# Second products of weight pairs run once for two token tiles, in products of 512 columns

## The chip, the cores and the metric

The program runs on one core of one Trainium2 chip. The core has five engines that run side by side and wait for each other through semaphores: TensorE (PE in the profile, its weight loads PEld), VectorE (DVE), ScalarE (ACT), GpSimd (POOL) and SyncE (SP), which issues the DMAs. The metric is the device time of one execution in microseconds (us); less is better.

## The reference

```python
# attention in chunks of 32 with 16 keys to the left, 8 to the right and 8 memory keys -> x [1536, 512]
# first layer: 4 experts, d = 512, f = 1024
p = domain_probs / (domain_probs.sum(-1, keepdims=True) + 1e-09)
for e in range(4):
    h = np.maximum(x @ w1[e], 0.0)
    out += p[:, e:e + 1] * (h @ w2[e])
# second layer: d = 512, f = 2048
h = x @ w_in
g = np.maximum(h, 0.0) + alpha * np.minimum(h, 0.0)
return (g @ w_out)
```

Everything is float32.

## The kernel before

The kernel keeps activations transposed: rows are features, columns are tokens. The 1536 tokens are two halves, a = 0 and a = 1, of 768 columns each (`NCOL`). A *token tile* is 384 columns of both halves, so there are two tiles, that with `c0 = 0` and that with `c0 = 384`. The hidden features come in 24 groups of 256, called p below: p = 0 to 15 are the experts of the first layer, four groups each, p = 16 to 23 are the second layer. Attention (12 units) runs ahead of and between the first tiles.

For each p and tile there are two products.

- The **first product** (`gemm1`) is a matrix product by seven block products (a scheme of the Strassen kind): groups of six matmuls into the PSUM banks a, b, d, a, c, d, c, 42 matmuls of 384 columns. Float32 is split in a high and a low part, and three matmuls (high by high, high by low, low by high) make one product. VectorE combines the banks between groups: `u`, `t`, `b`, `d`, `c` in the rows. The second c group adds into bank c, which VectorE must have read before (row `b<-c,t`).
- Then comes the nonlinearity (`gelu`), once for each of four blocks of the hidden features (i = 0, 1 by half a = 0, 1; block 2i+a), in the order 0, 3, 1, 2. It ends in an ACT cast that makes the high half of `gg` and a POOL subtraction that makes its low half (`gg<-g,gg`). In the second layer two ACT operations stand ahead of VectorE's.
- The **second product** (`gemm2`) multiplies the four blocks by the second weights: for each of four output blocks o and each half a, two features halves i by three matmuls, into one bank `y`; 48 matmuls of 384 columns. VectorE adds each bank to the accumulator `acc` (row `acc<-y,acc`).

Four groups around the change of layer (p = 14 to 17) go through `gemm2_two`, which already runs two p after two first products. The order of the program is the list `order`: (1, k) is the first product of tile k of the list `tiles`, (2, k) its second. For the other groups the list puts a first product ahead of the second product of the tile before it, as (1, k), (2, k-1).

Everything else is placed by hand into this order: a planner keeps a time `now`, which each matmul moves on, and generators (streams) emit a step when `now` reaches its due time. The streams are the preparation of the weights of the next p (stream "w": ACT casts `wh`, POOL subtractions `wl` and sums `s`) and the conversion of the second layer's float64 weights to float32 (stream "c": 32 chunks, in each five VectorE operations `fm`, `fm`, `fm`, `fw`, `fm` and two POOL operations `fl`). Each engine runs its instructions in the order in which they were emitted. All of this is recorded under line 61, so rows are told apart by their tiles.

Of the kernel before, what the change touches and what calls it, by code (L numbers as in the profile page):

```python
# [10 lines left out]
F32 = mybir.dt.float32  # L11
# [55 lines left out]
def tile_kernel(ctx: ExitStack, tc: tile.TileContext, qk, v, wa, wq, dpt, alpha, out):  # L67
# [77 lines left out]
    acc = xp.tile([P, KD, 2, NCOL], F32, name="acc")  # L145
# [12 lines left out]
    def prep_x(c0, n):  # L158
        cs = slice(c0, c0 + n)
        b11, b12 = acc[:, 0:2, 0, cs], acc[:, 0:2, 1, cs]  # L160
        b21, b22 = acc[:, 2:4, 0, cs], acc[:, 2:4, 1, cs]

        st = bp.tile([P, 3, 2, n], F32, tag="st", name=f"st{c0}")
        sub = ALU.subtract
        act.copy(xh[:, 0:4, cs], acc[:, :, 0, cs])
# [6 lines left out]
        pool.tensor_tensor(out=xl[:, 0:4, cs], in0=acc[:, :, 0, cs], in1=xh[:, 0:4, cs].bitcast(F32), op=sub)  # L172
        yield
        for z in (0, 1):
            r = slice(6 + 4 * z, 10 + 4 * z)
            t_ = st[:, z:z + 2].rearrange("p a b n -> p (a b) n")
            if z == 1:
                dve.tensor_tensor(out=st[:, 1], in0=b21, in1=st[:, 1], op=sub)
                yield
            act.copy(xh[:, r, cs], t_)  # L180
            if z == 0:
                pool.tensor_tensor(out=xl[:, 4:6, cs], in0=b22, in1=xh[:, 4:6, cs].bitcast(F32), op=sub)
            yield
            dve.tensor_tensor(out=xl[:, r, cs], in0=t_, in1=xh[:, r, cs].bitcast(F32), op=sub)
            yield
# [12 lines left out]
    qk_t = [bp.tile([P, QW + KW], F32, tag="ggB", bufs=4, name=f"qk{i}") for i in range(RING)]  # L198
# [28 lines left out]
    def unit(u):  # L227
# [62 lines left out]
        first = acc[:, :, 0, cols]  # L290
# [15 lines left out]
        dve.tensor_tensor(out=st[:, 0], in0=b12, in1=acc[:, 0:2, 0, cols], op=sub)  # L306
# [4 lines left out]
        dve.tensor_tensor(out=acc[:, 2:4, 1, cols], in0=st[:, 2], in1=b12, op=sub)  # L311
# [316 lines left out]
    glist = []  # L628
    lag = []
# [17 lines left out]
    def gemm1(p, c0, n, parity, last):  # L647
# [27 lines left out]
        gs = {}  # L675

        def gelu(blk, src):
# [12 lines left out]
            gg = bp.tile([P, 2, 384], F32R, tag="gg" + "AB"[parity], bufs=4, name=f"gg{blk}_{nm}")  # L690
            gh, gl = gg[:, 0, :n], gg[:, 1, :n]
# [49 lines left out]
    def gemm2(p, c0, n, gs, soon, last):  # L741
        prep_force("w", lambda: p in w2)
        wh, wl = w2[p]
        y = {}

        def part(o, ab, i, start, stop, z0=0, z1=n):
            lag_poll(lambda: 2 * i + ab in gs)
            gh, gl = gs[2 * i + ab]
            if start:
                y[o, ab] = bank(f"y{p}_{c0}_{o}_{ab}_{z0}")[:, :n]  # L750
            w_ = [x[:, 2 * i + o // 2, (o % 2) * P:(o % 2 + 1) * P] for x in (wh, wl)]
            for k, (a, b) in enumerate(((w_[0], gh), (w_[1], gh), (w_[0], gl))):
                product(y[o, ab][:, z0:z1], a, b[:, z0:z1], n=z1 - z0,
                        start=start and k == 0, stop=stop and k == 2)
            if stop:
                evac(p, c0 + z0, z1 - z0, o, ab, y[o, ab][:, z0:z1])

        tight = p == 0 and c0 + n < NCOL
        if tight:

            for o in range(2):
                part(o, 0, 0, True, False)
            for o in range(4):
                part(o, 1, 1, True, False)
                part(o, 1, 0, False, True)
            for o in range(2):
                part(o, 0, 1, False, True)
            for o in range(2, 4):
                part(o, 0, 0, True, False)
                part(o, 0, 1, False, True)  # L770
        elif soon:

            for o in range(4):
                part(o, 0, 0, True, False)
            for o in range(2):
                part(o, 1, 1, True, False)
            for o in range(4):
                part(o, 0, 1, False, True)
            for o in range(2):
                part(o, 1, 0, False, True)  # L780
        else:
            for o in range(4):
                part(o, 0, 0, True, False)
                part(o, 0, 1, False, True)
            for o in range(2):
                part(o, 1, 1, True, False)
                part(o, 1, 0, False, True)
        for o in () if tight else range(2, 4):

            end = p == NP - 1 and c0 + n == NCOL and o == 3  # L790
            for z0, z1 in ((0, n // 2), (n // 2, n)) if end else ((0, n),):
                part(o, 1, 1, True, False, z0, z1)
                part(o, 1, 0, False, True, z0, z1)
        if last:
            used2.add(p)
# [28 lines left out]
    def evac(p, c0, n, o, ab, src):  # L824
        dst = acc[:, o, ab, c0:c0 + n]
# [6 lines left out]
        if p == NP - 1:  # L832
            nc.sync.dma_start(out[o * P:(o + 1) * P, ab * NCOL + c0:ab * NCOL + c0 + n], dst)
# [52 lines left out]
    for i, (what, k, *other) in enumerate(order):  # L886
# [3 lines left out]
        if what == 1:  # L890
# [31 lines left out]
FIRST = [(0, 384), (384, 384)]  # L922
USE = (A11, S2, S1, A12, S3, S4, A22)
# [103 lines left out]
```

## Time and profile before

| | |
|---|---|
| three runs, median | 820.43 us (819.37 to 820.91) |
| span of the profiled execution | 817.4 us |
| around the span (820.43 - 817.4) | 3.0 us |
| TensorE busy | 801.4 us (98%) |
| VectorE busy | 584.5 us (72%) |
| GpSimd busy | 563.5 us (69%) |
| ScalarE busy | 330.8 us (40%) |
| DMA queue of the kernel | 70.75 MB, 26.9% of 16 engines |

The span goes from the first to the last instruction of the profiled execution. A matmul's row has its start and a modelled end; two matmuls that follow each other overlap, so the pace of the engine is read from the distance of starts.

### The profile page before, as it was taken

What the parts mean: (1) busy time and instruction counts of PE and PEld (TensorE: products, weight loads), DVE (VectorE), ACT (ScalarE), POOL (GpSimd) and SP (SyncE); (2) the same over time, 40 slices, a digit from 0 to 9 for tenths busy, and PEclk for the clock granted to TensorE, in tenths of its full rate; (3) what the DMA queues carried; (4) which work ended last, traced back from release to release, by engine and by line L of the source; (5) the groups of instructions that cost most, each with busy time, mean ns of one, the idle gap of its engine ahead of it and who ended that gap; (6) DMA issues with size and microseconds to landing.
All of it is one profiled execution on the core that took longest, in us unless ns stands there. A gap on an engine that the chain in (4) does not pass through costs nothing.

```text
span 817.4 us, 14838 instructions
## 1 busy us (share of the span) xinstructions
PE 801.4 (98%) x5637; PEld 787.0 (96%) x5637; DVE 584.5 (72%) x1116; ACT 330.8 (40%) x718; POOL 563.5 (69%) x587
## 2 busy tenths in 40 slices
PE   8889999999999999999999999999999999999998
PEld 6678999999999999999999999999899999999998
DVE  4777477777868768867777777587954877756555
ACT  3656523224133223232332323155672665456441
POOL 2867777777877877967887872293954987866611
PEclk9999999999999999999999999999999999999999
DMA  7882121331331431322432302001002142211004
GB/s 245 254 286 83 52 91 39 125 118 55 109 105 45 133 106 59 116 67 76 134 98 77 116 34 71 16 26 53 26 27 91 44 125 77 78 40 53 0 1 155
DMA packets 30503, 71.69 MB, mean 88 GB/s; under 512 B 4704, under 2 KB 9952, under 8 KB 30432
## 3 DMA queue, kind: packets, MB, share of 16 engines
q1 hardware_dynamic: 30432, 70.75, 26.9%
q8 instruction: 44, 0.72, 0.4%
q14 instruction: 27, 0.22, 0.1%
HBM read 59.18 MB, written 11.56 MB: 87 GB/s over the span
## 4 chain that ended last, share of the span: by engine, by line
PE 88%; DVE 3%; POOL 3%; ACT 2%; DMA 2%; issue 1%; SPq 0%; DVEq 0%; POOLq 0%; ACTq 0%
PE y L61 47%; PE a L61 11%; PE c L61 11%; PE d L61 11%; PE b L61 6%; DMA raw<-in_wa 2%; POOL gg L61 1%; DMA qk<-in_qk 1%; POOL s L61 1%; PE two L61 1%; PE x L61 1%; DVE pe L61 1%; DVE mx L61 0%; PE wps0.0_84 L61 0%; POOL wl L61 0%
## 5 line engine op out<-in xcount | busy, mean ns | idle before, releaser
L61 PE MATMUL y<-gg,wh 128*128 128x384 f32 x1540 | 397.7, 334 | 0.5 <-POOL gg L61 0.4
L61 POOL TENSOR_TENSOR gg<-g,gg 128x384 fp32r<-128x384 f32 x192 | 202.0, 1063 | 117.5 <-ACT gg L61 114.7
L61 PEld LDWEIGHTS y<-gg,wh 128*128 128x128 f32 x1540 | 278.3, 188 | 1.6 <-POOL gg L61 1.0
L61 PE MATMUL y<-gg,wl 128*128 128x384 f32 (+1 forms) x770 | 257.0, 334 | 0.0
L61 DVE TENSOR_TENSOR acc<-y,acc 128x384 f32<-128x384 f32 x321 | 172.0, 550 | 60.0 <-PE y L61 58.6
L61 ACT CAST gg<-g 128x384 fp32r<-128x384 f32 x192 | 97.6, 512 | 153.9 <-DVE g L61 153.7
L61 POOL TENSOR_TENSOR wl<-raw,wh 128x256 fp32r<-128x256 f32 (+1 forms) x112 | 114.0, 1026 | 49.8 <-ACT wh L61 36.1
L61 PEld LDWEIGHTS y<-gg,wl 128*128 128x128 f32 x770 | 144.5, 188 | 0.0
L61 ACT COPY u<-a 128x384 f32<-128x384 f32 x48 | 23.1, 481 | 194.2 <-PE a L61 194.2
L61 POOL TENSOR_TENSOR wl<-s,wh 128x256 fp32r<-128x256 f32 x88 | 68.5, 785 | 7.4 <-ACT wh L61 7.1
L61 DVE TENSOR_TENSOR u<-b,u 128x384 f32<-128x384 f32 x48 | 26.7, 556 | 60.6 <-PE b L61 57.8
L61 ACT CAST wh<-raw 128x256 fp32r<-128x256 f32 (+1 forms) x116 | 54.5, 491 | 17.6 <-PE y L61 14.7
L61 PE MATMUL d<-xh,wl 128*128 128x384 f32 x184 | 61.6, 335 | 0.0
L61 PE MATMUL d<-xl,wh 128*128 128x384 f32 x184 | 61.6, 335 | 0.0
L61 PE MATMUL d<-xh,wh 128*128 128x384 f32 x184 | 61.6, 335 | 0.0
L61 PE MATMUL a<-xh,wh 128*128 128x384 f32 x184 | 61.6, 335 | 0.0
L61 PE MATMUL a<-xl,wh 128*128 128x384 f32 x184 | 61.5, 334 | 0.0
L61 PE MATMUL a<-xh,wl 128*128 128x384 f32 x184 | 61.5, 334 | 0.0
L61 POOL TENSOR_TENSOR fl<-fl,fm 128x512 f32<-128x512 f32 x32 | 41.4, 1293 | 27.4 <-DVE fm L61 18.5
L61 PE MATMUL c<-xh,wh 128*128 128x384 f32 x176 | 59.3, 337 | 0.5 <-DVE b L61 0.5
L61 PE MATMUL c<-xh,wl 128*128 128x384 f32 x176 | 59.0, 335 | 0.0
L61 PE MATMUL c<-xl,wh 128*128 128x384 f32 x176 | 59.0, 335 | 0.0
(117 smaller groups left out, 1363.6 us busy)
## 6 DMA issues: line engine op xcount, KB each, us to landing
fr<-in_wq SPq DMA_DIRECT2D x32, 512.0 KB, 3.9
raw<-in_wa SPq DMA_DIRECT2D x28, 512.0 KB, 3.9
w2s<-fl SPq DMA_DIRECT2D x32, 256.0 KB, 2.4
raw<-w2s SPq DMA_DIRECT2D x16, 512.0 KB, 3.6
qk<-in_qk SPq DMA_DIRECT2D x24, 312.0 KB, 4.3
v<-in_v SPq DMA_DIRECT2D x48, 130.0 KB, 4.2
outT<-acc SPq DMA_DIRECT2D x15, 192.0 KB, 1.8
pb<-p_dram SPq DMA_DIRECT2D x6, 384.0 KB, 3.4
```

What stands on the lines that cost most here:

```text
L61: return self.tc.keep_in_program_order(f(*a, **kw))
```

## The change

Nineteen groups (the list `PAIRED`: all but p = 0 and p = 14 to 17) get a common second product for both tiles. Both first products of a p run one after the other, and then `gemm2_pair` runs the second product over 3 x 512 columns (j = 0, 2, 1) for each of four output blocks. For that the columns of `gg` and `acc` lie one after the other as tile, half, column: j = 0 is tile 0 (all of a = 0 and 128 columns of a = 1), j = 2 is in tile 1 alone, j = 1 lies across. p = 0 keeps a second product for each tile, right behind its own first product.

```diff
-    acc = xp.tile([P, KD, 2, NCOL], F32, name="acc")
+    half = NCOL // 2
+    acc = xp.tile([P, KD, 2, 2, half], F32, name="acc")
+    acc_all = acc.rearrange("p o t a n -> p o (t a n)")
...
+        wide = p in PAIRED
+        if not wide:
+            own = bp.tile([P, 2, 2, 2, half], F32R, tag="gg", bufs=2, name=f"gg_{nm}")
+
+        def gg_of(i, ab):
+            if not wide:
+                return own[:, i, 0, ab], own[:, i, 1, ab]
+            if (p, i) not in gg_t:
+                gg_t[p, i] = bp.tile([P, 2, 2, 2, half], F32R, tag="gg", bufs=2, name=f"gg_{p}_{i}")
+            return gg_t[p, i][:, 0, c0 // half, ab], gg_t[p, i][:, 1, c0 // half, ab]
...
-            gg = bp.tile([P, 2, 384], F32R, tag="gg" + "AB"[parity], bufs=4, name=f"gg{blk}_{nm}")
-            gh, gl = gg[:, 0, :n], gg[:, 1, :n]
+            gh, gl = gg_of(i, ab)
...
+    def gemm2_first(c0, n, gs, last):
...
+        for o in range(2):
+            part(o, 0, 0, True, False)
+        for o in range(4):
+            part(o, 1, 1, True, False)
+            part(o, 1, 0, False, True)
...
+    def gemm2_pair(p, gs):
+
+        prep_force("w", lambda: p in w2)
+        wh, wl = w2[p]
+
+        def chunk(o, j, z0, z1):
+            y = bank(f"y{p}_{o}_{j}_{z0}")[:, :z1 - z0]
+            cut = slice(j * 512 + z0, j * 512 + z1)
+            for i in range(2):
+                gh, gl = (gg_t[p, i][:, h].rearrange("p t a n -> p (t a n)")[:, cut] for h in range(2))
+                w_ = [x[:, 2 * i + o // 2, (o % 2) * P:(o % 2 + 1) * P] for x in (wh, wl)]
+                for k, (a, b) in enumerate(((w_[0], gh), (w_[1], gh), (w_[0], gl))):
+                    product(y, a, b, n=z1 - z0, start=i == 0 and k == 0, stop=i == 1 and k == 2)
+            dst = acc_all[:, o, cut]
+            dve.tensor_tensor(out=dst, in0=y, in1=dst, op=ALU.add)
+            if p == NP - 1:
+                nc.sync.dma_start(out[o * P:(o + 1) * P, cut], dst)
+
+        for j in (0, 2, 1):
+            for o in range(KD):
+                if o == 0:
+                    lag_poll(lambda: all(b in g for g in gs[:1 if j == 0 else 2] for b in range(4)))
+                end = p == NP - 1 and j == 1 and o == KD - 1
+                for z0, z1 in ((0, 256), (256, 512)) if end else ((0, 512),):
+                    chunk(o, j, z0, z1)
+        used2.add(p)
...
-    for k in range(k0 - 1):
+    for k in range(k0):
         order += [(1, k), (2, k)]
-    order += [(1, k0 - 1)]
-    for k in range(k0, kc + 1):
-        order += [(1, k), (2, k - 1)]
-    order += [(1, kc + 1), (2, kc, kc + 1)]
-    for k in range(kc + 2, kc + 8, 2):
+    for k in range(k0, len(tiles), 2):
         order += [(1, k), (1, k + 1), (2, k, k + 1)]
-    order += [(1, kc + 8)]
-    for k in range(kc + 9, len(tiles)):
-        order += [(1, k), (2, k - 1)]
-    order += [(2, len(tiles) - 1)]
```

Three places of the order of instructions. First TensorE, at the end of the first product of the second tile of p = 0 (`c0_384`); `a1_0` is the first product of p = 1. Before:

```order
L61 MATMUL c0_384_1489<-xl_106,wh1_0_6_864 128x384
L61 MATMUL c0_384_1489<-xh_105,wl1_0_6_865 128x384
L61 MATMUL a1_0_1536<-xh_105,wh1_1_0_1367 128x384
L61 MATMUL a1_0_1536<-xl_106,wh1_1_0_1367 128x384
L61 MATMUL a1_0_1536<-xh_105,wl1_1_0_1368 128x384
```

The same place after:

```order
L61 MATMUL c0_384_1483<-xl_106,wh1_0_6_861 128x384
L61 MATMUL c0_384_1483<-xh_105,wl1_0_6_862 128x384
L61 MATMUL y0_384_0_0_1526<-gg_0_384_1436,wh2_0_983 128x384
L61 MATMUL y0_384_0_0_1526<-gg_0_384_1436,wl2_0_984 128x384
L61 MATMUL y0_384_0_0_1526<-gg_0_384_1436,wh2_0_983 128x384
L61 MATMUL y0_384_1_0_1531<-gg_0_384_1436,wh2_0_983 128x384
```

The second product of this tile has moved from behind the first product of p = 1 to right behind its own first product.

Second VectorE, in the first product of the second tile of p = 8 (`u28_384`, `t8_384`, `b8_384`), before:

```order
L61 TENSOR_TENSOR acc_107<-y7_384_3_1_0_4129,acc_107 128x384
L61 TENSOR_TENSOR u28_384_4144<-b8_384_4146,u28_384_4144 128x384
L61 TENSOR_TENSOR t8_384_4165<-d8_384_4157,u28_384_4144 128x384
L61 SCALAR_TENSOR_TENSOR g0_8_384_4176<-a8_384_4137,pb2_384_3963 128x384
L61 TENSOR_SCALAR fm14_4181<-fr14_4092 128x512
L61 TENSOR_TENSOR b8_384_4146<-c8_384_4179,t8_384_4165 128x384
```

The same place after:

```order
L61 TENSOR_TENSOR c8_0_3808<-c8_0_3808,u28_0_3773 128x384
L61 SCALAR_TENSOR_TENSOR g2_8_0_3840<-c8_0_3808,pb2_0_3529 128x384
L61 TENSOR_SCALAR fm13_3845<-fr13_3754 128x512
L61 TENSOR_SCALAR fm13_3845<-fm13_3845 128x512
L61 TENSOR_TENSOR u28_384_3857<-b8_384_3859,u28_384_3857 128x384
L61 TENSOR_SCALAR fm13_3845<-fm13_3845 128x512
L61 TENSOR_TENSOR t8_384_3881<-d8_384_3872,u28_384_3857 128x384
L61 SCALAR_TENSOR_TENSOR fw13_3847<-fr13_3754,fm13_3845 128x512
L61 SCALAR_TENSOR_TENSOR g0_8_384_3893<-a8_384_3842,pb2_384_3761 128x384
L61 TENSOR_TENSOR b8_384_3859<-c8_384_3895,t8_384_3881 128x384
```

Ahead of `b8_384` stand now the end of the first tile's nonlinearity and four operations of a conversion chunk, where one stood before.

Third GpSimd, at the nonlinearity of the second tile of p = 19 (the four rows with `19_384`), before:

```order
L61 TENSOR_TENSOR wl1_20_0_7918<-raw0_20_7778,wh1_20_0_7917 128x256
L61 TENSOR_TENSOR fl28_7864<-fw28_7865,fl28_7864 128x512
L61 TENSOR_TENSOR wl1_20_1_7948<-s_20_7868,wh1_20_1_7947 128x256
L61 TENSOR_TENSOR gg0_19_384_7938<-g2_19_384_7937,gg0_19_384_7938 128x384
L61 TENSOR_TENSOR gg3_19_384_7963<-g3_19_384_7962,gg3_19_384_7963 128x384
L61 TENSOR_TENSOR wl1_20_2_7975<-s_20_7868,wh1_20_2_7974 128x256
L61 TENSOR_TENSOR gg1_19_384_7978<-g2_19_384_7937,gg1_19_384_7978 128x384
L61 TENSOR_TENSOR gg2_19_384_7986<-g2_19_384_7985,gg2_19_384_7986 128x384
```

The same place after:

```order
L61 TENSOR_TENSOR gg_19_0_7257<-g2_19_0_7256,gg_19_0_7257 128x384
L61 TENSOR_TENSOR wl1_20_0_7326<-raw0_20_7194,wh1_20_0_7325 128x256
L61 TENSOR_TENSOR gg_19_1_7285<-g2_19_0_7304,gg_19_1_7285 128x384
L61 TENSOR_TENSOR fl27_7268<-fl27_7268,fm27_7267 128x512
L61 TENSOR_TENSOR fl27_7268<-fw27_7269,fl27_7268 128x512
L61 TENSOR_TENSOR wl1_20_1_7361<-s_20_7261,wh1_20_1_7360 128x256
L61 TENSOR_TENSOR gg_19_0_7257<-g2_19_384_7356,gg_19_0_7257 128x384
L61 TENSOR_TENSOR gg_19_1_7285<-g3_19_384_7380,gg_19_1_7285 128x384
L61 TENSOR_TENSOR wl1_20_2_7389<-s_20_7261,wh1_20_2_7388 128x256
L61 TENSOR_TENSOR gg_19_0_7257<-g2_19_384_7356,gg_19_0_7257 128x384
L61 TENSOR_TENSOR gg_19_1_7285<-g2_19_384_7401,gg_19_1_7285 128x384
```

The last subtractions of the first tile and two operations of a conversion chunk stand now close ahead of the four of the second tile.

## Rows read from the trace of the kernel before

**Rows 1.** Page, busy time: us, share of the span, instructions.

```profile
PE 801.4 (98%) x5637; PEld 787.0 (96%) x5637; DVE 584.5 (72%) x1116; ACT 330.8 (40%) x718; POOL 563.5 (69%) x587
```

**Rows 2.** Chain of work that ended last: start us, us, what.

```profile
293.90 8.32 PE y L61 x48
302.22 1.04 PE a L61 x6
...
433.48 1.32 PE c L61 x6
```

**Rows 3.** Groups by shape: second products, high weights; count, busy us, mean ns.

```profile
L61 PE MATMUL y<-gg,wh 128*128 128x384 f32 x1532 | 396.4, 334 | 0.5 <-POOL gg L61 0.4
```

**Rows 4.** Timeline of TensorE at the end: start us, us, operation, count.

```profile
813.07 0.28 PE L61 MATMUL y<-gg,wl 128*128 128x192 f32 x1
...
813.40 0.28 PE L61 MATMUL y<-gg,wl 128*128 128x192 f32 x1
```

**Rows 5.** Timeline, TensorE: first product of p = 1 begins, tile 384 of p = 0 done.

```profile
83.66 0.33 PE L61 MATMUL a<-xh,wh 128*128 128x384 f32 x1
```

**Rows 6.** Timeline of GpSimd at that place.

```profile
84.15 1.02 POOL L61 TENSOR_TENSOR gg<-g,gg 128x384 fp32r<-128x384 f32 x1
85.12 1.30 POOL L61 TENSOR_TENSOR wl<-raw,wh 128x512 fp32r<-128x512 f32 x1
86.37 1.98 POOL L61 TENSOR_TENSOR gg<-g,gg 128x384 fp32r<-128x384 f32 x2
```

**Rows 7.** Timeline of all engines in the second tile of p = 5.

```profile
198.26 0.57 DVE L61 TENSOR_TENSOR b<-c,t 128x384 f32<-128x384 f32 x1 [0.43 <-PE c L61]
...
199.10 0.33 PE L61 MATMUL c<-xh,wh 128*128 128x384 f32 x1
```

**Rows 8.** Timeline after that tile: GpSimd and a conversion step on VectorE.

```profile
201.84 2.18 POOL L61 TENSOR_TENSOR gg<-g,gg 128x384 fp32r<-128x384 f32 x2
...
202.14 1.01 DVE L61 TENSOR_SCALAR fm<-fr 128x512 uint32<-128x512 uint32 x1
```

**Rows 9.** Timeline of all engines in `gemm2_two` of p = 16 and 17.

```profile
580.59 4.49 POOL L61 TENSOR_TENSOR gg<-g,gg 128x384 fp32r<-128x384 f32 x4
...
583.98 0.19 PEld L61 LDWEIGHTS y<-gg,wh 128*128 128x128 f32 x1 [0.47 <-POOL gg L61]
```

**Rows 10.** Timeline of VectorE, second tile of p = 18, right behind the first.

```profile
633.00 0.42 DVE L61 TENSOR_SCALAR fm<-fm 128x512 f32<-128x512 f32 x1
...
635.51 1.53 DVE L61 SCALAR_TENSOR_TENSOR fw<-fr,fm 128x512 uint32<-128x512 uint32 x1
636.97 0.55 DVE L61 TENSOR_TENSOR u<-b,u 128x384 f32<-128x384 f32 x1
637.44 0.54 DVE L61 SCALAR_TENSOR_TENSOR g<-c,g 128x384 f32<-128x384 f32 x1
...
638.37 1.24 DVE L61 TENSOR_SCALAR fm<-fw 128x512 uint32<-128x512 uint32 x1
639.53 0.55 DVE L61 TENSOR_TENSOR b<-c,t 128x384 f32<-128x384 f32 x1
```

**Rows 11.** Timeline of TensorE there: second c group, first second-product matmul.

```profile
640.14 0.45 PE L61 MATMUL c<-xh,wh 128*128 128x384 f32 x1 [0.29 <-DVE b L61]
...
641.31 0.33 PE L61 MATMUL y<-gg,wh 128*128 128x384 f32 x1
```

**Rows 12.** Timeline of GpSimd there: low halves of the four blocks.

```profile
644.46 2.00 POOL L61 TENSOR_TENSOR gg<-g,gg 128x384 fp32r<-128x384 f32 x2
646.42 0.73 POOL L61 TENSOR_TENSOR wl<-s,wh 128x256 fp32r<-128x256 f32 x1
647.12 2.16 POOL L61 TENSOR_TENSOR gg<-g,gg 128x384 fp32r<-128x384 f32 x2
```

**Rows 13.** Groups by shape: VectorE's conversion steps, count, busy us, mean ns.

```profile
L61 DVE SCALAR_TENSOR_TENSOR fw<-fr,fm 128x512 uint32<-128x512 uint32 x32 | 28.6, 895 | 0.1
...
L61 DVE TENSOR_SCALAR fm<-fw 128x512 uint32<-128x512 uint32 x32 | 17.4, 543 | 0.1
```

More of the change, by code (lines that the diff above doesn't have):

```diff
@@ L159, in prep_x @@
         cs = slice(c0, c0 + n)
-        b11, b12 = acc[:, 0:2, 0, cs], acc[:, 0:2, 1, cs]
-        b21, b22 = acc[:, 2:4, 0, cs], acc[:, 2:4, 1, cs]
+        top, low, every = slice(0, 2), slice(2, 4), slice(0, KD)
+        b11, b12 = acc_of(top, 0, c0, n), acc_of(top, 1, c0, n)
+        b21, b22 = acc_of(low, 0, c0, n), acc_of(low, 1, c0, n)
+        b1 = acc_of(every, 0, c0, n)
         st = bp.tile([P, 3, 2, n], F32, tag="st", name=f"st{c0}")
         sub = ALU.subtract
-        act.copy(xh[:, 0:4, cs], acc[:, :, 0, cs])
+        act.copy(xh[:, 0:4, cs], b1)
         dve.tensor_tensor(out=st[:, 0], in0=b12, in1=b11, op=sub)
@@ L195, in mm @@
         now[0] += took or 0.013 + n / 2.4e3
-    qk_t = [bp.tile([P, QW + KW], F32, tag="ggB", bufs=4, name=f"qk{i}") for i in range(RING)]
+    qk_all = bp.tile([P, RING, QW + KW], F32, tag="gg", bufs=2, name="qk")
+    qk_t = [qk_all[:, i] for i in range(RING)]
     v_t = [bp.tile([P, V_ROOM], F32, name=f"v{i}", **tag)[:, :VW].rearrange("p (e z w d) -> p e z w d", e=2, z=HP, w=NW)
@@ L289, in unit @@
         sub = ALU.subtract
-        first = acc[:, :, 0, cols]
+        a1, a2 = (acc_of(slice(0, KD), ab_, c * BLK, BLK) for ab_ in range(2))
+        first = a1
         if ab == 0:
@@ L645, in product, with gemm1 @@
         mm(*a, n=n, **kw)
[L647 removed]
+    def gemm1(p, c0, n, last):
         cs = slice(c0, c0 + n)
@@ L739, in gemm1, with part @@
         return gs
-    def gemm2(p, c0, n, gs, soon, last):
-        prep_force("w", lambda: p in w2)
-        wh, wl = w2[p]
+    def gemm2_first(c0, n, gs, last):
+        prep_force("w", lambda: 0 in w2)
+        wh, wl = w2[0]
         y = {}
-        def part(o, ab, i, start, stop, z0=0, z1=n):
+        def part(o, ab, i, start, stop):
             lag_poll(lambda: 2 * i + ab in gs)
@@ L749, in part @@
             if start:
-                y[o, ab] = bank(f"y{p}_{c0}_{o}_{ab}_{z0}")[:, :n]
+                y[o, ab] = bank(f"y0_{c0}_{o}_{ab}")[:, :n]
             w_ = [x[:, 2 * i + o // 2, (o % 2) * P:(o % 2 + 1) * P] for x in (wh, wl)]
             for k, (a, b) in enumerate(((w_[0], gh), (w_[1], gh), (w_[0], gl))):
-                product(y[o, ab][:, z0:z1], a, b[:, z0:z1], n=z1 - z0,
-                        start=start and k == 0, stop=stop and k == 2)
+                product(y[o, ab], a, b, n=n, start=start and k == 0, stop=stop and k == 2)
@@ L755, in part @@
             if stop:
[L756 to L793, printed above, removed]
-        if last:
-            used2.add(p)
+                evac(0, c0, n, o, ab, y[o, ab])
+        for o in range(2):
[3 more added lines that the diff above has]
+            part(o, 1, 0, False, True)
@@ new lines, in gemm2_first @@
+        for o in range(2):
+            part(o, 0, 1, False, True)
+        for o in range(2, 4):
+            part(o, 0, 0, True, False)
+            part(o, 0, 1, False, True)
+        if last:
+            used2.add(0)
+    def gemm2_pair(p, gs):
[21 more added lines that the diff above has]
+        used2.add(p)
@@ L831, in evac @@
             dve.tensor_tensor(out=dst, in0=src, in1=dst, op=ALU.add)
-        if p == NP - 1:
-            nc.sync.dma_start(out[o * P:(o + 1) * P, ab * NCOL + c0:ab * NCOL + c0 + n], dst)
-    half = NCOL // 2
     tiles = [(0, c0, n) for c0, n in FIRST]
     for p in range(1, NP):
-        if p not in (NP1 - 2, NP1 - 1, NP1, NP1 + 1):
+        if p in PAIRED:
             tiles += [(p, c0, half) for c0 in (0, half)]
@@ L911, in tile_kernel @@
             change[0] = kc - 1 <= k < kc + 8
-            acts[k] = gemm1(p, c0, n, k % 2, k == final[p])
+            acts[k] = gemm1(p, c0, n, k == final[p])
         else:
             change[0] = change[0] and k < kc + 6
-            if other:
+            if p == 0:
+                gemm2_first(c0, n, acts.pop(k), k == final[p])
+            elif p in PAIRED:
+                gemm2_pair(p, [acts.pop(k), acts.pop(k + 1)])
+            else:
                 gemm2_two(p, c0, n, [acts.pop(k), acts.pop(k + 1)], k == final[p])
-            else:
-                gemm2(p, c0, n, acts.pop(k), order[i - 1] == (1, k), k == final[p])
             if p == NP1 - 2:
@@ L922 @@
 FIRST = [(0, 384), (384, 384)]
+PAIRED = [p for p in range(1, NP) if p not in (NP1 - 2, NP1 - 1, NP1, NP1 + 1)]
 USE = (A11, S2, S1, A12, S3, S4, A22)
```

20 lines of the change are left out of this document (12 added, 8 removed).

## The prediction

> **What bounds the kernel now.** I read the page first, then the chain of waits, then timelines. TensorE is busy in 801.4 of 817.4 us [rows 1]. In the chain nearly every piece is TensorE, and its pieces touch: 48 matmuls of a second product take 8.32 us, and the next first product begins at the same moment [rows 2]. So TensorE's own pace sets the time: whatever takes time from its matmuls is gained in full, and whatever makes it wait is lost in full. The other engines matter only where they hand something over too late. VectorE's and GpSimd's shares (72% and 69%) do not bound anything by themselves, but both have stretches in which they are full.
>
> **Term 1, the matmuls.** 8.32 us by 48 is 173.3 ns for 384 columns [rows 2]. At the full clock of 2.4 GHz 384 columns are 160.0 ns, so each matmul has 13.3 ns on top. At 192 columns three matmuls start within 0.33 us, 110 ns each [rows 4], where 80.0 + 13.3 would be 93: below some 110 ns something else is the floor. No row has 512 columns. If the 13.3 ns belong to the instruction, such a matmul takes 213.3 + 13.3 = 226.7 ns. If they grow with the columns it takes 173.3 x 512/384 = 231.1. If they vanish it takes 213.3. I take 226.7: all rows of 384 columns, whatever they multiply, have the same pace, and each loads other weights than the one before it, which speaks for a price of the change of weights.
>
> The diff gives the counts. A pair had 2 x 48 = 96 matmuls and gets 3 x 4 x 6 = 72. In all 1818 of the 2298 of 384 columns (1532 with high weights, [rows 3]) and 12 of 192 become 1362 of 512 and 12 of 256. Before: 1818 x 0.1733 + 12 x 0.110 = 316.4 us. After: 1362 x 0.2267 + 12 x 0.120 = 310.2 us. **Gain 6.3 us**; 0.2 at 231.1 ns, 24.4 at 213.3 ns.
>
> The Trainium skill, "TensorE: Matmul & The Clock Gate", section "Back-to-back issue gap", has N/2.4 + 2.5 ns for a warm matmul. It would make 215.8 ns of 512 columns and a gain of some 21 us. The same rule gives 162.5 ns for 384 columns, and the trace has 173.3, so here the trace disagrees with it.
>
> **Term 2, the second tile of p = 0.** Its second product now follows its own first product with nothing between. In the trace that first product ends at 83.66 [rows 5]. Six matmuls on block 0 reach to 84.70. Then come three on block 3, the third of which needs the low half that GpSimd has ready at 84.15 + 1.02 = 85.17 [rows 6]; due at 85.05, it waits 0.1. Then block 1, whose third matmul is due at 85.69. GpSimd does a weight subtraction of 1.30 first and has block 1 ready at 86.37 + 0.99 = 87.36 [rows 6]: a wait of 1.7. GpSimd's order there is unchanged, so nothing shortens it. Behind the waiting matmul stands all of TensorE. **Cost 1.8 us**, between 1.5 and 2.1.
>
> **Term 3, a shorter cover for the last nonlinearity.** Before, 48 matmuls (8.3 us) of the other tile lay between a first product and the first use of its blocks. Now it is chunk j = 0, 24 x 0.2267 = 5.44 us. The third matmul of j = 2 (5.9 us after the first product's end) needs the low half of block 1, GpSimd's third; the sixth (6.6 us) that of block 2, its fourth. In the first layer this is hidden: in p = 5 the first product ends at 199.10 + 1.04 = 200.14 [rows 2, 7], and the last two low halves end at 201.84 + 2.18 = 204.02 [rows 8], 3.9 us later. In the second layer two more ACT steps stand in the chain. For p = 18 the first product ends at 641.31 [rows 11]; GpSimd's third ends about 648.2, 6.9 us later, the fourth at 649.28, 8.0 us later [rows 12]. That was hidden by 8.3 us; now it costs 1.0 and then 0.4 us. p = 18 already ran two first products in a row, so this reading carries over. For p = 19 to 21 the order has about one row of 0.73 us less ahead of these [rows 12]: third at 6.2, fourth at 7.2, waits of 0.3 and 0.4, so 0.7 each. p = 22 and 23 have no conversion left and stay hidden. **Cost 1.4 + 2.0 = 3.4 us**; at least 1.4, at most four times 1.4. That such a wait is real is seen in the groups that were paired before: there the low halves ran until 585.1, and TensorE's load waited 0.47 us at 583.98 [rows 9].
>
> **Term 4, VectorE in the second first product of a pair.** The link with least slack is bank c: VectorE's `b` starts at 198.26, lasts 0.57, and the second c group starts at 199.10 [rows 7], so 0.27 us are spare. `b` starts 0.84 before that group, hence 1.24 after its own group's start, with groups of 1.04 [rows 2]. Counted from the tile's start, `u`, `t`, the first nonlinearity and `b` can begin at 2.28, 3.32, 4.36 and 5.40, and the second c group is due at 6.24. Operations that read PSUM follow each other 0.47 apart (636.97 to 637.44, [rows 10]). New is that the first tile's last two operations run until 1.14. That leaves gaps of 1.14, 0.57, 0.57 and 0.57 us. Into them fall, by the order, conversion steps of a chunk: in p = 4 to 11 three to five ahead of `b`, in p = 8 two, one, one and none.
>
> What a step takes is open. Free it takes 0.42 (at 633.00, [rows 10]); the means go from 0.54 to 0.90 [rows 13]. It takes 1.01 when it starts at 202.14 while GpSimd is in an operation that began at 201.84 and lasts about 1.05: it ends 0.3 after GpSimd's end [rows 8]. The Trainium skill, "SBUF — State Buffer", section "Who interferes with whom", says that VectorE and GpSimd share a port pair as an exclusive lock for a whole instruction; the trace agrees, with the 1.01 us. By it every step that meets a running GpSimd operation waits it out. In p = 8 with steps of about 0.6 to 0.9, `b` is on time: no wait. With 1.0 for each, it starts 0.86 + 0.43 + 0.43 - 0.57 = 1.15 late, a wait of 0.9. GpSimd is fuller here, since eight low halves fall into the same stretch; p = 18 before shows it, with steps of 1.53 and 1.24 [rows 10] and TensorE idle for 0.29 and late by another 0.1 [rows 11]. I take 0.2 for each of eight pairs, nearer to the means: **cost 1.6 us**, between 0 and 7.2.
>
> **What costs nothing.** VectorE's 16 additions for a pair become 12 longer ones, hidden under chunks of 1.36 us. The first write of the next pair into a `gg` buffer comes four groups (4.2 us) after the last read, so the two buffers don't make anything wait; without that distance a nonlinearity chain would stand behind the matmuls. Weight preparation sees two first products close together and then 16 us of second product, more room than before. The output DMAs are fewer and larger, of which only the last is seen, below 0.2 us. One stall goes: at 433.48 a c group took 1.32 instead of 1.04 [rows 2], in a tile which is now the first of its pair: 0.3 back.
>
> **Sum.** -6.3 + 1.8 + 3.4 + 1.6 - 0.3 = +0.2 us on a span of 817.4, with the 3.0 around it unchanged: 820.6 against the median of 820.4. My forecast is that the gain on the matmuls is eaten by new waits. A measurement of this kernel tells about 0.2% (1.6 us) from no change.
>
> **Rivals.** *VectorE falls behind in the pairs (slower).* If most steps in p = 4 to 11 meet a running GpSimd operation, each pair loses 0.6 instead of 0.2, 3.2 us more: 823.8. It decides from 0.4 a pair. For it speaks p = 18; against it, that chunks fell into single first products before, too, and cost 0.3 at 433.48 [rows 2]. *The waits stay away (faster).* If the steps meet an idle GpSimd, term 4 is nothing, and if GpSimd is through earlier in p = 19 to 21, term 3 is 1.4: 820.6 - 1.6 - 2.0 = 817.0. For it speaks p = 5, where GpSimd is through 3.9 us after the first product [rows 7, 8]; against it p = 18. *The extra grows with the columns (slower).* At 231.1 ns the gain is 0.2: 826.7. *The skill's spacing (faster).* At 215.8 ns the second products take 293.9 + 1.3 = 295.2 us, 15.0 less than in the sum: 805.6; the row of 384 columns speaks against it.
>
> **Chances.** Forecast (within 0.2%) 0.32; VectorE behind 0.28; extra by columns 0.07; waits away 0.28; skill's spacing 0.05. So slower 0.35, same 0.32, faster 0.33. The range of 816 to 826 leaves out the last of these, most of the 826.7 and the tails of term 4.
>
> **What would show it.** Starts of 512-column matmuls 226.7 ns apart prove term 1. A wait of TensorE for GpSimd's `gg` of 1.7 us about 3 us after the first product of p = 0's second tile proves term 2; waits of 0.3 to 1.0 us some 5.9 us after the second first product in p = 18 to 21, and none in p = 22 and 23, prove term 3. Waits `c` for VectorE's `b` in p = 4 to 11 give term 4. Wrong I am if the spacing differs by more than 2 ns (each is 1.4 us per ns), or if the waits of terms 3 and 4 add up to less than 3 or more than 7 us.

## The result and the profile after

The changed kernel takes 826.71 us (median of 4 runs, 825.71 to 828.21) against 820.67 for the kernel before on the same chip: ratio 1.0077, 95% interval 1.0058 to 1.0096. A later repetition, c_after below, gave 1.0094 (1.0082 to 1.0106). It is slower, by about 0.8%.

The page of the changed kernel, what answers to [rows 1] and [rows 3]:

```profile
PE 805.3 (98%) x5181; PEld 730.5 (88%) x5181; DVE 577.9 (70%) x1040; ACT 328.5 (40%) x718; POOL 563.5 (68%) x587
...
L61 PE MATMUL y<-gg,wh 128*128 128x512 f32 (+1 forms) x1236 | 368.7, 376 | 5.1 <-POOL gg L61 4.9
...
L61 PE MATMUL a<-xh,wh 128*128 128x384 f32 x184 | 62.3, 338 | 0.3 <-ACT u L61 0.2
```

TensorE's share is as before and tells nothing. The last column does: the idle time for GpSimd's `gg` was 0.4 us in [rows 3] and is 4.9, and TensorE now waits for ACT's copy `u`, of which the waits before have no row.

The chain of waits at the end, to be held against [rows 2], shows what an undisturbed pair takes (start us, us, what):

```profile
774.14 1.04 PE c L61 x6
775.18 16.36 PE y L61 x72
791.54 1.06 PE a L61 x6
```

72 matmuls in 16.36 us are 227.2 ns each. To see where time is lost I read the start of every first product from the timeline of TensorE. In the kernel before the starts are 15.60 us apart, two tiles 31.20. After, a pair takes 7.31 + 23.64 = 30.95 where nothing waits. What a stretch takes above that is called its extra; a wait's size is the distance of two starts less the usual one (the wait column shows less, since it counts from a modelled end that lies behind the next start).

| part of the stretch | predicted, us | measured, us |
|---|---|---|
| nineteen pairs, 31.20 to 30.95 each | -6.3 | -4.75, and -0.2 for the split last group |
| second tile of p = 0 | +1.8 | +1.95 |
| last nonlinearity, p = 18 to 21 | +3.4 | 1.5 + 1.7 + 1.4 + 0.8 = +5.4 |
| handovers in the second first product | +1.6 (p = 4 to 11) | +4.5 (p = 8 to 13: 0.34, 0.88, 0.61, 1.01, 0.81, 0.89) |
| p = 15, first tile | none | +1.0 |
| stalls that went | -0.3 | -0.7 |
| sum | +0.2 | +7.2 |

The stretch runs from the start of the first product of p = 0's second tile to the end of the last matmul: 738.1 us before, 745.3 after. That is 7.2 us, while the medians lie 6.0 apart here and 8.5 in c_after. What lies ahead of the stretch is the same program, but it varies: that start lies between 75.4 and 81.2 us in thirteen profiles, of the changed kernel and of the experiments, which don't differ up to there. So stretches are compared below beside the times.

**p = 0.** TensorE's timeline, then GpSimd's (start, us, what):

```profile
86.59 0.34 PE L61 MATMUL y<-gg,wl 128*128 128x384 f32 x1
88.32 0.61 PE L61 MATMUL y<-gg,wh 128*128 128x384 f32 x2 [1.39 <-POOL gg L61]
```

```profile
86.03 1.28 POOL L61 TENSOR_TENSOR wl<-raw,wh 128x512 fp32r<-128x512 f32 x1
87.27 1.97 POOL L61 TENSOR_TENSOR gg<-g,gg 128x384 fp32r<-128x384 f32 x2
```

As in [rows 6], a weight subtraction stands ahead of block 1's low half; TensorE starts 1.55 us late behind it, and with the small delays around it 1.95 us go.

**p = 13**, second tile (first product from 477.16). VectorE:

```profile
475.75 1.09 DVE L61 TENSOR_SCALAR fm<-fm 128x512 f32<-128x512 f32 x1
476.76 0.55 DVE L61 SCALAR_TENSOR_TENSOR g<-b,pb 128x384 f32<-128x384 f32 x1
477.23 0.55 DVE L61 TENSOR_TENSOR d<-d,u 128x384 f32<-128x384 f32 x1
477.69 0.41 DVE L61 TENSOR_SCALAR fm<-fm 128x512 uint32<-128x512 uint32 x1
...
479.08 0.56 DVE L61 SCALAR_TENSOR_TENSOR g<-c,pb 128x384 f32<-128x384 f32 x1
479.55 1.21 DVE L61 SCALAR_TENSOR_TENSOR fw<-fr,fm 128x512 uint32<-128x512 uint32 x1
480.80 1.12 DVE L61 TENSOR_SCALAR fm<-fw 128x512 uint32<-128x512 uint32 x1
481.84 0.54 DVE L61 TENSOR_TENSOR u<-b,u 128x384 f32<-128x384 f32 x1
482.49 0.56 DVE L61 TENSOR_TENSOR t<-d,u 128x384 f32<-128x384 f32 x1
```

GpSimd, ACT and TensorE in the same stretch:

```profile
475.55 1.01 POOL L61 TENSOR_TENSOR gg<-g,gg 128x384 fp32r<-128x384 f32 x1 [2.13 <-ACT gg L61]
477.99 1.02 POOL L61 TENSOR_TENSOR gg<-g,gg 128x384 fp32r<-128x384 f32 x1 [1.43 <-ACT gg L61]
479.20 2.44 POOL L61 TENSOR_TENSOR gg<-g,gg 128x384 fp32r<-128x384 f32 x2 [0.19 <-ACT gg L61]
```

```profile
479.67 0.51 ACT L61 CAST gg<-g 128x384 fp32r<-128x384 f32 x1 [0.55 <-DVE g L61]
480.09 0.47 ACT L61 COPY u<-a 128x384 f32<-128x384 f32 x1
```

```profile
480.11 0.34 PE L61 MATMUL d<-xh,wl 128*128 128x384 f32 x1
480.61 0.45 PE L61 MATMUL a<-xh,wh 128*128 128x384 f32 x1 [0.17 <-ACT u L61]
480.90 0.34 PE L61 MATMUL a<-xl,wh 128*128 128x384 f32 x1
481.07 0.33 PE L61 MATMUL a<-xh,wl 128*128 128x384 f32 x1
...
482.63 0.34 PE L61 MATMUL c<-xh,wl 128*128 128x384 f32 x1
483.11 0.45 PE L61 MATMUL d<-xh,wh 128*128 128x384 f32 x1
```

Conversion steps (`fm`, `fw`) stand between VectorE's last operations for the first tile. So its last `g` comes at 479.08, ACT's cast of it at 479.67, and only behind that cast ACT copies bank a to `u`. The second a group wants bank a at 480.28 and starts at 480.61. Two more steps delay VectorE's own `u` and `t`, and the second d group starts 0.30 late as well.

**p = 18** (first product from 637.61 to 645.76, with 0.85 us of waits for VectorE in it, as before in [rows 11]), GpSimd and TensorE, for [rows 12]:

```profile
645.59 1.30 POOL L61 TENSOR_TENSOR fl<-fl,fm 128x512 f32<-128x512 f32 x1
646.98 1.30 POOL L61 TENSOR_TENSOR fl<-fw,fl 128x512 f32<-128x512 f32 x1
648.23 0.74 POOL L61 TENSOR_TENSOR wl<-raw,wh 128x256 fp32r<-128x256 f32 x1
648.92 2.00 POOL L61 TENSOR_TENSOR gg<-g,gg 128x384 fp32r<-128x384 f32 x2
650.88 0.75 POOL L61 TENSOR_TENSOR wl<-s,wh 128x256 fp32r<-128x256 f32 x1
651.58 2.15 POOL L61 TENSOR_TENSOR gg<-g,gg 128x384 fp32r<-128x384 f32 x2
```

```profile
651.47 0.39 PE L61 MATMUL y<-gg,wl 128*128 128x512 f32 x1
652.64 0.74 PE L61 MATMUL y<-gg,wh 128*128 128x512 f32 x2 [0.78 <-POOL gg L61]
...
653.79 0.50 PE L61 MATMUL y<-gg,wh 128*128 128x512 f32 x1 [0.17 <-POOL gg L61]
```

The last low half ends at 653.73, 8.0 us after the first product, and its user follows at 653.79. Two `fl` and weight subtractions stand ahead, and GpSimd runs from the first `fl` on with hardly a gap. In p = 19 TensorE's first matmul behind the first product and GpSimd's last two low halves are:

```profile
678.27 0.39 PE L61 MATMUL y<-gg,wh 128*128 128x512 f32 x1
```

```profile
684.23 2.15 POOL L61 TENSOR_TENSOR gg<-g,gg 128x384 fp32r<-128x384 f32 x2
```

The last one ends 8.1 us after the first product.

### The profile page after: what moved, and what is told of

Its sections match the earlier page's. It is cut to its first block, busy times and chain, and to the rows that moved or that the text cites. A ratio compares the mean times of both kernels' runs of the same rounds, so it can differ in the third digit from the quotient of the medians.

```text
span 825.7 us, 13798 instructions
## 1 busy us (share of the span) xinstructions
PE 805.3 (98%) x5181; PEld 730.5 (88%) x5181; DVE 577.9 (70%) x1040; ACT 328.5 (40%) x718; POOL 563.5 (68%) x587
## 5 line engine op out<-in xcount | busy, mean ns | idle before, releaser
L61 PE MATMUL y<-gg,wh 128*128 128x512 f32 (+1 forms) x1236 | 368.7, 376 | 5.1 <-POOL gg L61 4.9
L61 PEld LDWEIGHTS y<-gg,wh 128*128 128x128 f32 x1236 | 228.8, 188 | 44.6 <-POOL gg L61 9.6
L61 DVE TENSOR_TENSOR acc<-y,acc 128x512 f32<-128x512 f32 (+2 forms) x245 | 165.5, 678 | 101.5 <-PE y L61 100.0
L61 PE MATMUL y<-gg,wl 128*128 128x512 f32 (+1 forms) x618 | 231.9, 375 | 0.0
L61 POOL TENSOR_TENSOR wl<-raw,wh 128x256 fp32r<-128x256 f32 (+1 forms) x112 | 112.2, 1015 | 42.4 <-ACT wh L61 40.5
L61 PEld LDWEIGHTS y<-gg,wl 128*128 128x128 f32 x618 | 116.1, 188 | 17.5
```

Source lines behind the costliest of these rows:

```text
L61: return self.tc.keep_in_program_order(f(*a, **kw))
```

## The experiments

The theory: the width gives less than predicted, and the rest is waits that can be taken away one by one. The rivals stand with each run. Each ratio is against runs of the kernel before on the same chip (their medians lie between 819.85 and 820.67); stretch and extras, in us, are from each run's profile.

| kernel | time, us | ratio to before (95%) | stretch | p = 8 to 13 | p = 15 | p = 18 to 21 |
|---|---|---|---|---|---|---|
| before | 820.67 | 1 | 738.1 | - | - | - |
| changed | 826.71 | 1.0077 (1.0058 to 1.0096) | 745.3 | 4.5 | 1.0 | 6.3 |
| c_after (the same) | 828.37 | 1.0094 (1.0082 to 1.0106) | 745.0 | 4.5 | 1.0 | 6.1 |
| e1_width | 830.84 | 1.0124 (1.0096 to 1.0152) | 748.1 | 2.6 | 0.4 | 4.6 |
| e2_no_conv | 823.02 | 1.0028 (1.0013 to 1.0044) | 740.6 | 0.0 | 0.9 | 6.3 |
| e3_no_wprep | 829.33 | one run | 745.7 | 4.8 | 1.4 | 6.1 |
| e4_u_first | 825.47 | 1.0057 (1.0038 to 1.0075) | 741.4 | 1.4 | 0.1 | 6.1 |
| e4_again | 823.76 | 1.0050 (1.0037 to 1.0062) | 741.4 | 1.3 | 0.1 | 6.0 |
| e5_lows_last | 822.75 | 1.0032 (1.0015 to 1.0049) | 740.3 | 4.5 | 1.0 | 1.4 |
| e6_p0_cover | 825.69 | 1.0073 (1.0044 to 1.0102) | 743.0 | 4.6 | 1.0 | 6.0 |
| e8_no_conv_late | 822.81 | 1.0034 (1.0017 to 1.0052) | 740.2 | 4.5 | 1.0 | 1.3 |
| e10_phase | 823.50 | 1.0045 (1.0032 to 1.0058) | 740.5 | 0.0 | 1.0 | 6.1 |
| e9_all_late | 814.13 | 0.9933 (0.9910 to 0.9957) | 731.7 | 0.0 | 0.0 | 0.0 |
| e11_narrow_clean | 820.12 | 1.0002 (0.9989 to 1.0015) | 736.8 | 0.0 | 0.0 | 0.0 |

In p = 18 to 21, 0.95 us were there before (in the first products of p = 18 and a little in 19 and 20).

**The width alone.**

```diff
-            cut = slice(j * 512 + z0, j * 512 + z1)
+            cut = slice(j * 384 + z0, j * 384 + z1)
...
-        for j in (0, 2, 1):
+        for o, j in [(o, 0) for o in range(4)] + [(0, 1)] + [(o, 3) for o in range(4)] + [(o, 2) for o in range(4)] + [(o, 1) for o in (1, 2, 3)]:
```

> The second products of the nineteen pairs run in 384 columns instead of 512, in the same order over tiles and with nearly the same cover (30 matmuls of tile 0 ahead of tile 1, 5.20 us instead of 5.44). Theory (an extra per instruction, as the changed kernel's spacings say: 227.4 ns at 512 columns, 173.4 at 384): a pair takes 96 x 173.4 - 72 x 227.4 ns = 0.27 us more, 19 pairs 5.2 us, and the waits of p = 18 to 21 grow by 0.24 each: about 832.5 against 826.7 of the changed kernel. Rival (the extra grows with the columns, so the width gives nothing): only the 1.0 of the shorter cover, 827.5.

An undisturbed pair takes 31.20 us instead of 30.95: the width is worth 0.25 us a pair. The time (830.84) lies between the theory's 832.5 and the rival's 827.5; it went up by less than 4.75, because the waits also moved: they lie in p = 5 to 8 and 10 to 13 here (0.49, 0.87, 0.45, 0.80, 0.85, 0.65, 0.19 and 0.11). They didn't grow in p = 18 to 21, as I had expected, but shrank: a 384-column group of half a = 1 wants blocks 1 and 3 first, and block 2 only four groups later. So this run tells the width, but not by its total.

**No conversion in the second first product.** A list `muted` keeps a stream from emitting.

```diff
     def prep_poll():
-        for name in list(streams):
+        for name in [x for x in streams if x not in muted]:
...
+            muted[:] = ['c'] if p in PAIRED and p < NP1 and c0 else []
             acts[k] = gemm1(p, c0, n, k == final[p])
+            muted[:] = []
```

> The conversion stream emits nothing during the second first product of the pairs p = 1 to 13; its steps come in the second product and in the next first product of tile 0 instead. Theory (the three to five conversion steps that VectorE runs there make its handovers late): the extra time of p = 8 to 13 over an undisturbed pair (0.34, 0.88, 0.61, 1.01, 0.81 and 0.89 us, together 4.5) falls to below 0.6 in all, while the 1.0 us in p = 15 and the waits of p = 18 to 21 stay: 822.2. Rival 1 (VectorE is full there anyway, by the first tile's last operations and GpSimd's low halves): more than half of the 4.5 stays, above 824.4. Rival 2 (the steps only move their waits to the first product of tile 0): the pairs' periods stay as they are, 826.7.

Every pair from p = 1 to 13 now takes 30.95. All of the 4.5 us goes with the conversion steps, those on VectorE and the `fl` on GpSimd together, and they cost nothing where they went. Both rivals fall.

**No weight preparation instead.** The same with `muted[:] = ['w'] if p in (8, 10, 12) and c0 else []`.

> The weight preparation (GpSimd's subtractions, ACT's casts) emits nothing during the second first product of p = 8, 10 and 12; p = 9, 11 and 13 are left as they are and serve for comparison. Rival of the conversion theory (VectorE's steps are long because GpSimd runs weight subtractions at the same time, or ACT's casts are in the way of u): the extra of p = 8, 10 and 12 (0.34, 0.61, 0.81 us) falls below 0.3 in each. Conversion theory: the number of VectorE's steps is the same and the first tile's low halves still run on GpSimd, so at least 0.25, 0.4 and 0.5 stay. The total hardly tells, below 1.2 us of gain either way; the periods of the pairs do.

The extras of p = 8, 10 and 12 are 0.17, 0.62 and 0.74; the unmuted ones 0.91, 1.15 and 1.21. The first misses the line of the theory (0.25), the other two hold it. GpSimd and VectorE in p = 12 (first product from 446.89):

```profile
447.65 3.17 POOL L61 TENSOR_TENSOR gg<-g,gg 128x384 fp32r<-128x384 f32 x3 [0.55 <-ACT gg L61]
```

```profile
449.02 0.94 DVE L61 TENSOR_SCALAR fm<-fm 128x512 uint32<-128x512 uint32 x1
450.05 1.32 DVE L61 SCALAR_TENSOR_TENSOR fw<-fr,fm 128x512 uint32<-128x512 uint32 x1
...
451.77 0.41 DVE L61 TENSOR_SCALAR fm<-fw 128x512 uint32<-128x512 uint32 x1
```

No weight subtraction runs, and the steps are still long: 0.94 and 1.32 beside GpSimd's three low halves, 0.41 when they are over.

**`u` ahead of the casts.**

```diff
-        hold[0] = p >= NP1
+        hold[0] = p >= NP1 or p > 0 and c0 > 0 or p == NP1 - 1
```

> In the second first product of each pair, and in p = 15, ACT's copy u of bank a is emitted ahead of the casts that are still due for the first tile. Theory (the waits a<-u arise because u stands on ACT behind a cast that waits for VectorE's late last nonlinearity of the first tile): the a waits of p = 9, 11, 12, 13 and 15 (0.15, 0.38, 0.18, 0.45 and 0.99 us, together 2.1) go, and with u earlier also part of the d waits of p = 11 to 13 (0.39, 0.58, 0.41): 823.5 to 824.6. Rival (VectorE itself is late, and u only the first to show it): the waits come back at the d and c groups, less than 0.8 is gained, above 825.9.

All a waits went, that of p = 15 too, and most of the d and c waits with them: the stretch is 3.9 us shorter, more than I had expected. The edit also puts the casts behind `u`, and so GpSimd's low halves, later; how the gain beyond the 2.1 us of a waits divides between the two is not shown. Small c waits came in p = 2 and 7 (0.27 and 0.21). The time had gained only 1.2, so it was run again:

> The kernel of e4_u_first once more, since its two measures do not agree: in its profile the stretch from the start of p = 1 to the last matmul is 3.9 us shorter than in the changed kernel (723.8 instead of 727.7), while its time was only 1.2 us below. If the part behind p = 1 is what the edit changes and the start varies between runs by itself, the stretch is again 723.8 within 0.2 and the median over more runs comes to 822.8 or a little above. If the edit itself makes the start longer, the time stays at about 825.5.

The stretch is the same to 0.1 us, and the median over six more runs is 823.76. The edit does what the stretch says. In the first profile the start came at 81.2 us, the latest of all; that this also raised the first median of six runs is likely, but one profile doesn't show it.

**The changed kernel again.**

> The changed kernel itself, unaltered, for a second profile and more times. The stretch from the start of p = 1 to the last matmul should be 727.7 within 0.2 us again with the same waits; the start of p = 1 itself (94.84 us in the first profile) may differ by some us, as it did between 92.9 and 98.8 in kernels which are the same up to there; the median 826 to 828.

The stretch and the waits of p = 8 to 15 come out the same to 0.3 us. From the start of p = 1 (94.26) it is 727.4, a little outside the 0.2, and the median of 828.37 lies above the 828 expected. Part of the difference is p = 19, where 1.5 us go instead of 1.7.

**Shifting the conversion.**

```diff
-                streams["c"][0] = now[0] + 20.0
+                streams["c"][0] = now[0] + 24.0
```

> One number: the conversion stream begins 24 instead of 20 us after the start of p = 1, so that its chunks, whose distance is a little less than a pair's period, drift into the second first products of the pairs later. Nothing is left out. By the order, the steps lie in p = 12 and 13 where they lie in the changed kernel in p = 6 and 7, which had no wait. Theory (the waits arise where two or more steps fall between the last 2.4 us of the first tile's first product and the first 2 us of the second's): the extra of p = 8 to 13, 4.5 us, falls to at most 0.5, that of p = 2 to 7 rises to at most 0.6 (in p = 2 to 5 one or two steps lie ahead of the border): 822.3 to 823.3. Rival (later pairs have their waits from something else that grows, such as GpSimd's or ACT's queue): at least 2.5 of the 4.5 us stays in p = 8 to 13.

No pair from p = 1 to 13 has an extra above 0.04 us; the time, 823.50, is just above the expected range. So nothing in the later pairs is fuller than in the earlier ones; it is where the steps fall. By the planner's time two chunks take about 1 us less than a pair, so the steps come earlier from pair to pair, until they reach the border between the two first products. In the changed kernel's trace a chunk's first step starts 4.9 us behind this border in p = 2, 1.3 behind it in p = 6 and 7, and 2.4 ahead of it in p = 13; here it is 1.3 behind in p = 13. Four microseconds of delay put that off until behind p = 13.

**Low halves last, in j = 2.**

```diff
+            if p >= NP1 and j == 2:
+                lag_poll(lambda: all(b in g for g in gs for b in range(4)))
+                lows_last(j)
+                continue
```

`lows_last` opens four banks, runs the two high matmuls of both i for each o, and then the low ones with the additions.

> In the second layer's pairs (p = 18 to 23) the columns j = 2 run with all sixteen matmuls on high halves first, in four open banks, and the eight on low halves behind them. Theory (TensorE waits there for GpSimd's last two low halves, and only for these): the first low half is wanted 5.46 + 16 x 0.227 = 9.1 us after the first product, behind the last one's end (8.8 us in p = 18, 8.1 in p = 19), so the waits of 1.51, 1.64, 1.37 and 0.76 us in p = 18 to 21 go: -5.3, 821.4 against 826.7. Rival (ACT's casts of the high halves are as late): TensorE waits at the start of j = 2 instead, 0.3 to 1.0 us in each, and less than 3 us are gained.

No wait for `gg` is left in p = 18 to 21; what is left is 0.86 in p = 18 and 0.56 in p = 19, which are waits for VectorE inside their first products. The stretch is 4.9 us shorter. (The 8.8 us for p = 18 in the expectation are 8.0, since its first product ends late.) The high halves were there in time, so the rival falls.

**No conversion late.** The list again, with `['c'] if p >= NP1 + 2 and c0 else []`.

> The conversion stream emits nothing during the second first product of p = 18 to 21 (elsewhere as in the changed kernel): the two fl operations, 2.6 us on GpSimd, and one to three VectorE steps come later, in the second product. Theory (the last low halves are late because GpSimd's queue has these fl operations ahead of them): the low halves come up to 2.6 us earlier, the waits of p = 18 to 21 (1.51, 1.64, 1.37, 0.76) fall to at most 0.2 each, and with the VectorE steps also the 0.85 us in the first product of p = 18 goes: 821.0. Rival (the second layer's longer chain on ACT, or GpSimd's weight subtractions, sets it): at least half of the 5.3 stays, above 823.2.

6.3 us fell to 1.3 (0.56, 0.23, 0.24, 0.25), not to the 0.8 or less of the theory. GpSimd in p = 18 (first product until 644.03), ACT and VectorE:

```profile
647.16 1.19 POOL L61 TENSOR_TENSOR wl<-s,wh 128x256 fp32r<-128x256 f32 x1
648.84 2.18 POOL L61 TENSOR_TENSOR gg<-g,gg 128x384 fp32r<-128x384 f32 x2 [0.49 <-ACT gg L61]
```

```profile
648.25 0.98 ACT L61 CAST gg<-g 128x384 fp32r<-128x384 f32 x2 [0.82 <-DVE g L61]
```

```profile
646.64 1.11 DVE L61 SCALAR_TENSOR_TENSOR fw<-fr,fm 128x512 uint32<-128x512 uint32 x1
647.67 0.55 DVE L61 SCALAR_TENSOR_TENSOR g<-d,g 128x384 f32<-128x384 f32 x1
```

The last low half ends at 651.02, 7.0 us after the first product instead of 8.0. Now GpSimd waits 0.49 for ACT, and ACT's casts wait 0.82 for VectorE's last two `g`, which stand behind the conversion step `fw` that was put off. So the fifth that is left is, at least in part, not the longer chain of the second layer: in p = 22, where no conversion is left, the same chain ends 5.8 us after the first product. The edit takes the `fl` from GpSimd and the steps from VectorE at once and doesn't tell them apart; that GpSimd's queue was the late one in the changed kernel is read from its rows in p = 18 above.

**More cover in p = 0.** For the second tile the order of use is block 0 for four o, block 3 for three, then block 1.

```diff
+            for o in range(4):
+                part(o, 0, 0, True, False)
+            for o in range(3):
+                part(o, 1, 1, True, False)
+            for o in range(3):
+                part(o, 1, 0, False, True)
```

> In the second product of the second tile of p = 0 all four output blocks begin with block 0, then three with block 3, and only then block 1 is used: its low half is wanted 21 matmuls and two more (4.0 us) after the first product instead of 2.0. Theory (only the order of use makes this wait): the 1.94 us of the four delays there fall to at most 0.2, 824.9 against 826.7; the stretch from the start of that first product to the start of p = 1 falls from 17.55 to 15.6 to 15.8 us. Rival (seven open banks at once: the banks of the first product come free too late, so TensorE waits for VectorE instead): at least 1.0 us stays. The start before it varies by some us between runs, so the stretch tells more than the total.

The stretch to p = 1 is 15.60 us, so all 1.95 are gone; seven open banks did no harm. The total (825.69) can hardly show it.

**All together, and without the width.**

> All together: no conversion steps in the second first product of any pair, ACT's copy u ahead of the due casts, lows last in j = 2 of the second layer, and the longer cover in p = 0. If the waits are what the single runs make them, independent of each other: -4.7 (p = 8 to 13), -0.9 (p = 15), -5.3 (p = 18 to 21), -0.8 (first product of p = 18) and -1.9 (p = 0), together -13.6: 813.1, and 7.5 below the kernel before. Rival (taken away here, they come back at other handovers, as in the first product of the next pair, which now gets the conversion steps): less than 9 us of gain, above 817.7.

The stretch is 13.6 us shorter, as the sum of the single edits said; the time, 814.13, is 12.6 below that of the changed kernel. The chain in p = 13 has no gap (start us, us, what):

```profile
478.95 1.04 PE c L61 x6
479.99 16.36 PE y L61 x72
496.36 1.06 PE a L61 x6
```

This version beats both kernels, by 0.7% the one before. The same with 384 columns, both halves of tile 0 first and no lows-last:

> As e9_all_late, but with second products in 384 columns, both halves of tile 0 first (48 matmuls, 8.3 us of cover), so that no lows-last order is needed. It shows what the width alone is worth where no wait covers it. By the periods (31.20 us with 384 columns in e1_width, 30.95 with 512) 19 x 0.25 = 4.75 us slower than e9_all_late: 818.9, 1.2 below the kernel before. Rival (the pairing without the width already gives e9's gain, since without waits TensorE has slack to hide the difference): within 1.5 us of 814.1.

820.12 us, no difference from the kernel before and 1.2 more than I had expected; its stretch is 5.1 us longer than that of e9_all_late. Its pairs take 31.20, those of e9_all_late 30.95. So the pairing by itself gives no time that these runs can tell; the width does, where no wait eats it.

## Why the prediction was wrong

The result lies just outside the range. Of the two conditions that the prediction gave for being wrong, one is met: the spacing was near (227.2 ns, not 2 off), but the waits of terms 3 and 4 add up to 9.9 us instead of 5, over the bound of 7. That new waits eat the gain on the matmuls was right; terms 3 and 4 were too small, and the waits of p = 15 were no term.

**Term 1** had the right mechanism, the extra belongs to the instruction. It was mis-sized by 1.4 us: 72 matmuls take 16.36 us instead of 16.32, and a first product behind a 512-column one takes 7.31 instead of 7.28. (Its own numbers give 6.2 and not 6.3.) The rival of 231.1 ns is excluded by the pairs' periods in e1_width and e11_narrow_clean; that the time falls on this rival's 826.7 is chance. That the extra is a price of the change of weights is not shown: in a first product the first two of each three matmuls have the same `wh`, and they follow each other at the same 173 ns. The Trainium skill, "TensorE: Matmul & The Clock Gate", "Back-to-back issue gap", has a formula for an isolated warm matmul that would make 215.8 ns; this stream, with a weight load for each matmul, has 227.2 and disagrees at 512 columns as it did at 384.

**Term 2** was right: 1.95 for 1.8, at the predicted place.

**Term 3** was right for p = 18 (1.5 for 1.4, with the last low half 8.0 us after the first product, as read) and in that p = 22 and 23 have none. The step that failed is "for p = 19 to 21 the order has about one row of 0.73 us less ahead of these". In p = 19 the first product ends at 678.29 and the last low half at 686.38, 8.1 us later instead of the 7.2 that I had worked out; in p = 20 it is 7.8, and in p = 21 7.2, with the wait of 0.8 that belongs to this. So 3.9 us came in p = 19 to 21 instead of 2.0. GpSimd's queue with the two `fl` was the late one, by its rows; e8_no_conv_late takes most of it away with the conversion, and e5_lows_last shows that only low halves were late. In c_after the last low half of p = 19 comes at 7.3, but 0.5 us are lost inside the first product instead.

**Term 4** failed most: 4.5 us for 1.6, and in p = 8 to 13 for p = 4 to 11. Three steps were wrong. First, "the first tile's last two operations run until 1.14": in p = 5, with no step between them, the last one starts 0.85 us after the border between the two first products and ends at 1.41; in p = 13, with conversion steps between them, it starts at 1.92 and ends at 2.48. Second, I followed only `b`. What is queued behind the late nonlinearity on ACT is the cast, and behind the cast `u`, which frees bank a and which VectorE's own `u` reads; with `u` first, in e4_u_first, 4.1 of the 5.5 us in p = 8 to 15 are gone. Third, "0.2 for each of eight pairs" spread evenly what depends on phase, as e10_phase shows. The rows of VectorE by tile, first of the stretch of p = 2 to 7 and then of p = 8 to 13 (duration ns min/median/max, first and last start):

```profile
L61 DVE TENSOR_SCALAR fm<-fm x25: 408/494/1195, 125.2 to 306.9; 128x512 uint32<-128x512 uint32 x13, 128x512 f32<-128x512 f32 x12
...
L61 DVE TENSOR_SCALAR fm<-fm x22: 410/887/1124, 321.1 to 477.7; 128x512 f32<-128x512 f32 x11, 128x512 uint32<-128x512 uint32 x11
```

The median goes from 494 to 887 ns: nearer the border the steps meet the first tile's low halves on GpSimd. In e10_phase, where the steps lie further behind the border, both medians are 420 ns. The Trainium skill, "SBUF — State Buffer", "Who interferes with whom", calls VectorE's and GpSimd's port pair an exclusive lock, and the trace agrees: in p = 13 the step at 475.75 takes 1.09 us, 0.20 us behind the start of a low half, and that at 477.69, which starts while GpSimd is idle, 0.41. The rival "VectorE falls behind" (823.8) named this, and its 4.8 us for eight pairs are near the 4.5 measured; what it lacks is the rest of term 3, of term 1 and p = 15.

**p = 15** was no term at all. It is the same link on ACT: 1.0 us, gone with `u` first.

The 3.0 us "around it, unchanged" were not what lies around a span. Later runs of the kernel before show 1.8 us around it (819.29 us with a span of 817.5); by that the profiled run was one of the faster ones. This moves no term, but a profile's span should be set beside its own run's time.

## What to carry to other kernels

When two stages are put back to back, list for every engine what stands in its queue at their border, not only the operands that the next stage reads: here a copy that frees a bank stood behind a cast that stood behind background work. Background work that runs at its own period drifts against the stages, so a stretch that is free of waits in one trace tells little of the same stretch with another period; look at where its steps fall in each repetition, or keep them out of the tight window by rule. A small saving per instruction on the bounding engine is real (4.75 us here), but here it showed only when the waits that the new order makes were taken away.

## What was not expected of the hardware

A matmul that starts late by a wait is followed by one that is late too: 0.29 us behind it (480.61 to 480.90) where 0.173 is usual. Nearly all waits from p = 0's second tile on have this, 0.10 to 0.11 us each, so that a wait costs TensorE that much more than the waiting itself.

A 512-column matmul with a weight load of its own is paced at 227.2 ns, 14 more than 512 columns at 2.4 GHz (the granted clock is 0.996 of that and more), about the same addition as at 384 columns (13.3). At these two widths it is a price of the instruction and not of the column.
